# One load per tensor for each chunk of 1024 tokens, with a new written order of work

## The chip, the cores and the metric

The kernel runs on one core of a Trainium2 chip. A core has five engines that run side by side, each with its own list of instructions: PE (matrix products; its weight loads are shown apart, as PEld), DVE (vector), ACT (functions of one element), POOL (a second vector engine) and SP, which here only issues transfers. 16 DMA engines move data between device memory (HBM) and the core's memory (SBUF). PE writes its results to PSUM, a small memory of 8 banks of 2 KB for each of the 128 partitions. An engine takes its instructions strictly in order; an instruction whose input isn't there holds up all behind it on that engine. The metric is the time of one execution on the device in microseconds (us), as the median of several runs. One profiled execution shows where the time goes.

## The reference

The input is `x` with two gates, `r_gate` and `i_gate`, each of 4 sequences x 6336 tokens x 256 channels in float32, so 25,344 tokens in all. Two layers follow each other.

```python
sig_r, sig_i = sigmoid(r_gate), sigmoid(i_gate)
a_t  = exp(8 * sig_r * log(sigmoid(a_param)))          # one decay per token and channel
gx   = sqrt(max(1 - a_t * a_t, 1e-6)) * sig_i * x
for t in range(S):                                     # along each sequence
    h = a_t[:, t] * h + gx[:, t];  y[:, t] = h
gate = sigmoid(causal depthwise convolution of y with conv_w, 5 taps)
out  = (gate * (y @ w_val)) @ w_out                    # w_val, w_out: 256 x 256
```

## The kernel before

**Units.** Tokens are cut into 51 *tiles* (`wins`: 512 tokens, a few of 256) and the tiles are joined into 28 *chunks* (`CHUNKS`): the first three and the last two are single tiles, the 23 between are pairs, 1024 tokens. Channels are two halves of 128 (`h`). Pairs of chunks may form a *group* (`GROUPS`) for the transposes and Exp of the decay, and up to three chunks a *batch* (`BATCHES`) for the square roots.

**Layouts.** Loads put tokens on partitions: a tile of 512 tokens lies as 128 partitions x 4 tokens x 256 channels, four successive tokens in one partition, so one piece of a transfer is 4 x 256 x 4 bytes = 4 KB. The scan along the tokens needs channels on partitions, so PE transposes in between. Pairs of bf16 values travel as one float32 through such transposes.

**The steps.** Each has a two-letter name in the order; the line is that of the profile before.

- `lr`, `li`, `lx`: loads of the gates and of x, one tile and tensor each (512 KB), by SP (L274). Gates go to `riring` with places for 4 tiles (`NRI`), x to `xring` with 4 (`NX`).
- `th`: ACT takes Tanh of both gates of a tile at once into `tring` (bf16, L289). `tring` has 3 places (`NTRI`) of three parts: the i-gate always lies in the middle part and the r-gate alternates between the outer two (`swapped`), so that an r-part is overwritten only by the tile six later, an i-part by the tile three later.
- `tr`, `ex`: PE transposes the r-gate's Tanh (L334), ACT makes the decay from it by Exp into `aring` (L350).
- `sq` (or `sa` on ACT), `rt`: POOL squares the decay into `ering` (L358), ACT takes the square root of 1 - a^2 of a whole batch at once (L377). The square root needs another function table on ACT, so a batch costs two table loads (L509).
- `nt`, `xg`: PE transposes the root back to token layout (L392); DVE multiplies it into `uring` (L399).
- `pp` and `up` on POOL (L297, L309), or `xp` on PE with `uv` on DVE (L314, L323): the product of the i-gate and x, into `uring`.
- `xt`, `sc`: PE transposes the gated input to channel layout in PSUM (L408); DVE runs the scan into `yring` (L430).
- `cv`, `tg`: the convolution as 20 small products on PE (L442) and its Tanh on ACT (L449); `vl`, `gv`: the value product on PE (L457) and the gating on DVE (L462).
- `ou`, `cd` or `ca`, `st`: the output product on PE (L472), its copy to `oring` on DVE (L480) or ACT (L482), and the store by SP (L493).

In `nt`, the transposes of one tile pick every second float of `ering`, since a partition of token layout holds four successive tokens as two pairs; `xt` writes with the same step into PSUM:

```python
in_=ering[:, e + q:e + wins[w] // 2:nq]        # nt, nq = 2 for 512 tokens
out=bank[:, o + q:o + wins[w] // 2:nq]         # xt
```

**The order.** Nothing is scheduled by a compiler. The string `ORDER` lists every step (`th.7` is Tanh of tile 7; `tr.3.1@0,1` names PSUM banks), and the loop at L504 emits them one after the other, each to its engine. So each engine's list is the order of its own steps in the string; the place of a step relative to those of other engines has no effect beyond which data it must wait for. All loads and stores share SP's list: a store that waits for its copy holds up the loads behind it.

Of the kernel before, what the change touches and what calls it, by code (L numbers as in the profile page):

```python
# [26 lines left out]
NTRI = 3  # L27
# [6 lines left out]
s_ident s_small s_kt s_diag li.2 lr.2 th.2 lr.3 lr.0 li.0 th.0 pp.0 tr.2.0@0 li.1 lr.1 tr.0.0@1 ex.2.0 th.1 lx.0 lx.2  # L34
li.3 up.0 tr.2.1@2 ex.2.1 tr.0.1@0 ex.0.0 tr.1.1@3 ex.1.1 tr.1.0@4 sq.1.1 ex.0.1 sq.0.1 lx.3 xp.3@0,1 lx.1 lr.6 th.3
sq.0.0 rt.0 lr.5 sq.2.0 pp.2 up.2 nt.0@5 xg.0 xt.0@2,3 li.5 th.5 sq.2.1 li.6 lr.4 uv.3 th.6 pp.6 pp.5 xp.1@5 sc.0.0
sc.0.1 cv.0@2,3 uv.1 li.4 th.4 tg.0 s_wl.1 ex.1.0 lx.4 li.7 tr.3.1@0,1 s_wl.0 lr.7 ex.3.1 lx.5 tr.3.0@2,3 ex.3.0
s_wl.3 lx.6 lx.7 pp.4 up.4 th.7 lr.9 rt.2 xp.7@2,3 li.8 uv.7 sa.4.0 sq.4.1 sq.3.1 sq.1.0 rt.1 nt.2@0 xg.2 nt.1@1 xg.1
s_wl.2 lr.8 li.10 lx.8 xt.2@2,3 xt.1@0,1 sc.1.1 li.9 lr.10 sq.3.0 rt.3 li.11 up.6 sc.1.0 lx.10 lr.11 sc.2.1 sc.2.0
up.5 th.8 lx.11 s_wcast th.10 lx.9 pp.10 up.10 lr.14 th.9 li.13 li.14 lr.13 xp.8@4,5 li.12 lr.12 uv.8 th.11 li.15  # L40
nt.3@0,1 xg.3 nt.4@6,7 pp.11 up.11 cv.1@2,3 tg.1 xg.4 xt.3@0,1 sc.3.1 vl.1@4,5 tr.5.0@6,7 ex.5.0 sq.5.0 tr.5.1@2,3
gv.1 ou.1.0@1 cd.1.0 st.1 lx.12 lr.15 ex.5.1 vl.0@4,5 xp.9@6,7 th.14 sq.5.1 cv.2@2,3 sc.3.0 th.13 uv.9 lx.13 xt.4@1,0
gv.0 ou.0.0@4 cd.0.0 st.0 sc.4.1 lx.15 cv.3@6,7 th.12 li.16 li.18 tr.7.1@4,5 tg.2 vl.2@2,3 gv.2 tg.3 ex.7.1 sq.6.1
sq.6.0 lx.14 pp.14 pp.12 up.12 tr.7.0@6,7 ex.7.0 sq.7.0 lx.16 cv.4@2,3 tg.4 th.15 ou.2.0@4,5 cd.2.0 sc.4.0 st.2 lr.18
lr.16 vl.3@6,7 xp.13@2,3 vl.4@4,5 gv.4 sq.7.1 rt.4 uv.13 th.16 sq.8.1 sq.8.0 pp.15 up.15 li.17 lr.17 up.14 ou.4.0@4,5
li.19 cv.5@0,1 lr.19 gv.3 cd.4.0 lx.17 tg.5 ou.3.0@6,7 lx.18 st.4 cd.3.0 st.3 nt.5@4,5 li.20 xg.5 pp.16 up.16 th.17
pp.17 lr.20 nt.7@6,7 xg.7 lx.19 li.21 nt.6@2,3 xg.6 th.18 pp.18 lr.21 xt.5@4,5 sc.5.1 up.17 vl.5@6,7 cv.6@0,1 tg.6
th.19 tr.9.1@2,3 ex.9.1 li.22 lr.22 up.18 sq.9.1 pp.19 gv.5 sc.5.0 tr.9.0@6,7 ex.9.0 lx.20 ou.5.0@0,1 cd.5.0 sq.10.1
xt.6@5,4 up.19 sc.6.1 cv.7@0,1 tg.7 cv.8@2,3 th.20 lr.24 tg.8 sc.6.0 vl.6@6,7 gv.6 xt.7@0,1 cv.9@4,5 ou.6.0@6,7 sc.7.0
th.21 tg.9 cd.6.0 vl.7@2,3 gv.7 vl.9@6,7 th.22 tr.11.0@0 sc.7.1 ou.7.0@2,3 vl.8@4,5 sq.9.0 tr.12.0@1 gv.9 ou.9.0@6,7  # L50
gv.8 ou.8.0@4,5 sq.10.0 st.5 cd.7.0 cd.9.0 lx.22 st.6 rt.5 lx.21 nt.8@6,7 lr.23 li.23 cd.8.0 nt.9@4,5 pp.22 pp.21
up.22 pp.20 up.20 up.21 xg.8 ex.12.0 xg.9 ex.11.0 li.24 st.7 st.9 li.25 lr.25 lx.23 lx.24 li.26 lr.26 th.23 xt.8@6,7
sc.8.0 sq.11.0 pp.23 sq.12.0 lr.27 li.27 cv.11@2,3 tg.11 cv.10@4,5 sc.8.1 cv.12@0,1 st.8 th.24 pp.24 tg.10 tg.12
vl.11@2,3 tr.11.1@6 ex.11.1 gv.11 vl.10@4,5 gv.10 th.25 xt.9@0,1 sc.9.0 tr.12.1@2 ex.12.1 ou.11.0@6,7 cd.11.0
# [45 lines left out]
def kernel(  # L100
# [46 lines left out]

    segs, y_at, y_wrap = [], [], []
    at = 4
# [33 lines left out]
    with tc.manual_schedule():  # L183
# [79 lines left out]
        def swapped(w):  # L263

            return (w // NTRI) % 2

# [274 lines left out]
```

## Time and profile before

| | |
|---|---|
| median of 3 runs | 301.58 us (300.14 to 303.82) |
| profiled execution | 300.32 us, of which 298.5 us from the first to the last instruction (the span) |
| busy: ACT, DVE, PE, POOL | 278.8, 247.6, 246.4, 232.8 us |
| moved by DMA | 104.75 MB, 351 GB/s over the span |
| PE's granted clock | 0.977 of full speed |
| landing of a 512 KB load | 8.0 to 8.3 us after its issue (median) |

In the profile's groups, a line names the source line, engine and operation, the written and the read buffers, then busy time and mean duration, then the idle time of the engine just before these instructions with what ended most of it. Times in the slices are tenths of each fortieth of the span. The *chain that ended last* follows the work back from the last instruction: at each step to what released it. Its shares say where a delay would have moved the end.

### The profile page before, as it was taken

To read this page: it belongs to the slowest core of one execution; us is meant where nothing else is said; L and a number is where in the kernel's file an instruction comes from. 1 tells how busy PE (TensorE), PEld (TensorE's weight loads), DVE (VectorE), ACT (ScalarE), POOL (GpSimd) and SP (SyncE) were. 2 spreads that over 40 slices of the span, in tenths; PEclk is the share of its full clock that TensorE was granted. 3 is DMA by queue.
4 is the path that set the end of the run, shared out by engine and by line. 5 is a ranking of instruction groups with operands and counts; after the bars stand their busy time and mean duration, and the time that the engine had idled before them with its cause. 6 is when DMAs were issued, how large, how long until landed. Compare 5 with 4: busy or idle time off the path is not lost.

```text
span 298.5 us, 6286 instructions
## 1 busy us (share of the span) xinstructions
PE 246.4 (83%) x2509; PEld 167.8 (56%) x2509; DVE 247.6 (83%) x206; ACT 278.8 (93%) x197; POOL 232.8 (78%) x155
## 2 busy tenths in 40 slices
PE   0374577897888598989898899998979999899993
PEld 0134255454556466757664758567647675666662
DVE  2030288849999889999999999999999899899993
ACT  6799999999999999999999999999999999969863
POOL 1478958989999899899999879998995996255300
PEclk9997599999999979999999999999999999999999
DMA  6999999999999999999999998999999977726046
GB/s 252 408 408 385 379 411 407 406 414 406 337 379 370 419 416 415 411 406 321 417 411 375 388 417 335 396 353 361 349 409 419 408 278 270 273 116 248 29 186 246
DMA packets 29995, 104.75 MB, mean 351 GB/s; under 512 B 3335, under 2 KB 3854, under 8 KB 29966
## 3 DMA queue, kind: packets, MB, share of 16 engines
q1 hardware_dynamic: 29952, 104.35, 90.5%
q8 instruction: 19, 0.31, 0.4%
q14 instruction: 10, 0.08, 0.1%
q10 hardware_dynamic: 14, 0.01, 0.0%
HBM read 78.39 MB, written 25.95 MB: 350 GB/s over the span
## 4 chain that ended last, share of the span: by engine, by line
ACT 31%; PE 23%; DVE 13%; issue 13%; DMA 12%; POOL 5%; SPq 1%; ACTq 0%; DVEq 0%; POOLq 0%
ACT tring L289 10%; ACT aring L350 8%; DMA riring<-in_r_gate_dram 7%; DVE yring L430 7%; PE banks L442 5%; ACT tgring L449 5%; PE banks L457 5%; ACT ering L377 4%; PE banks L472 4%; PE banks L392 3%; DMA riring<-in_i_gate_dram 3%; DVE tgring L462 3%; DVE oring L480 2%; DMA xring<-in_x_dram 2%; ACT L509 2%
## 5 line engine op out<-in xcount | busy, mean ns | idle before, releaser
L430 DVE TENSOR_TENSOR_SCAN yring<-aring,yring,banks 128x1024 bf16<-128x1024 f32 (+5 forms) x54 | 106.2, 1988 | 0.9 <-PE banks L408 0.6
L358 POOL TENSOR_TENSOR ering<-aring 128x1024 f32<-128x1024 f32 (+2 forms) x54 | 91.5, 1713 | 9.7 <-ACT aring L350 9.7
L309 POOL TENSOR_TENSOR uring<-tring,xring 128x1024 bf16<-128x1024 bf16 (+1 forms) x45 | 94.6, 2113 | 4.9 <-DMA xring<-in_x_dram 3.5
L289 ACT ACTIVATE tring<-riring 128x2048 bf16<-128x2048 f32 (+1 forms) x51 | 93.8, 1867 | 4.1 <-DMA riring<-in_i_gate_dram 1.9
L297 POOL TENSOR_SCALAR tring<-tring 128x1024 bf16<-128x1024 bf16 (+1 forms) x45 | 45.8, 1026 | 30.5 <-ACT tring L289 30.4
L442 PE MATMUL banks<-yring,diag 64*64 64x512 bf16 (+7 forms) x1080 | 61.9, 361 | 4.6 <-ACT aring L350 1.6
L462 DVE SCALAR_TENSOR_TENSOR tgring<-tgring,banks 128x1024 bf16<-128x1024 bf16 (+1 forms) x51 | 58.9, 1178 | 5.5 <-PE banks L457 4.4
L472 PE MATMUL banks<-wo,tgring 128*128 128x256 bf16 x396 | 51.4, 274 | 4.7 <-DVE tgring L462 3.5
L350 ACT ACTIVATE aring<-banks,khf 128x2048 f32<-128x2048 bf16 (+3 forms) x38 | 54.1, 1474 | 0.5 <-PE banks L334 0.4
L449 ACT ACTIVATE tgring<-banks 128x1024 bf16<-128x1024 f32 (+1 forms) x51 | 50.4, 1009 | 3.4 <-PE banks L442 3.3
L457 PE MATMUL banks<-yring,wv 128*128 128x512 bf16 (+4 forms) x216 | 49.4, 361 | 5.0 <-DVE oring L480 2.2
L472 PEld LDWEIGHTS <-tgring 128*128 128x128 bf16 x396 | 41.0, 114 | 15.7 <-DVE tgring L462 9.6
L442 PEld LDWEIGHTS <-diag 64*64 64x64 bf16 x1080 | 30.3, 106 | 28.8 <-issue 13.6
L377 ACT ACTIVATE ering<-ering 128x4096 bf16<-128x4096 f32 (+5 forms) x15 | 44.9, 3019 | 0.1
L399 DVE TENSOR_TENSOR uring<-banks,uring 128x2048 bf16<-128x2048 bf16 (+2 forms) x28 | 29.8, 1095 | 18.2 <-PE banks L392 17.9
L480 DVE COPY oring<-banks 128x1024 f32<-128x1024 f32 (+1 forms) x35 | 40.6, 1181 | 4.8 <-ACT aring L350 2.4
L334 PE MATMUL banks<-ident_b,tring 128*128 128x128 bf16 x396 | 29.0, 227 | 12.2 <-ACT tring L289 10.4
L334 PEld LDWEIGHTS <-tring 128*128 128x128 bf16 x396 | 25.1, 101 | 17.7 <-ACT tring L289 11.7
L457 PEld LDWEIGHTS <-wv 128*128 128x128 bf16 x216 | 19.7, 97 | 26.3 <-issue 12.4
L392 PE MATMUL banks<-ident,ering 128*128 128x128 f32 x198 | 28.8, 296 | 6.8 <-DVE oring L480 2.6
L392 PEld LDWEIGHTS banks<-ident,ering 128*128 128x128 f32 x198 | 25.9, 208 | 13.5 <-ACT ering L377 7.7
L408 PE MATMUL banks<-ident,uring 128*128 128x128 f32 x198 | 27.5, 282 | 2.6 <-DVE uring L399 2.5
(36 smaller groups left out, 113.1 us busy)
## 6 DMA issues: line engine op xcount, KB each, us to landing
riring<-in_i_gate_dram SPq DMA_DIRECT2D x48, 512.0 KB, 8.2
riring<-in_r_gate_dram SPq DMA_DIRECT2D x48, 512.0 KB, 8.3
xring<-in_x_dram SPq DMA_DIRECT2D x48, 512.0 KB, 8.0
out_dram<-oring SPq DMA_DIRECT2D x48, 512.0 KB, 5.7
riring<-in_r_gate_dram SPq DMA_DIRECT2D x3, 256.0 KB, 6.3
riring<-in_i_gate_dram SPq DMA_DIRECT2D x3, 256.0 KB, 6.5
xring<-in_x_dram SPq DMA_DIRECT2D x3, 256.0 KB, 5.3
out_dram<-oring SPq DMA_DIRECT2D x3, 256.0 KB, 7.3
```

Of the source, the lines that this page charges most:

```text
L289: nc.scalar.activation(out=tring[:, w % NTRI, a:a + 2, 0:J, :], in_=riring[:, w % NRI, :, 0:J, :], func=ACT.Tanh, scale=0.5)
L309: nc.gpsimd.tensor_tensor(out=u, in0=t1, in1=xt, op=ALU.mult)
L350: nc.scalar.activation(out=dst, in_=src, func=ACT.Exp, scale=khf[:, h:h + 1], bias=khf[:, h:h + 1])
L358: nc.gpsimd.tensor_tensor(out=e, in0=a, in1=a, op=ALU.mult)
L377: nc.scalar.activation(out=ering[:].bitcast(BF16)[:, 4 * o:4 * o + 2 * n], in_=ering[:, 2 * o:2 * o + 2 * n], func=ACT.Sqrt, scale=-0.25, ...
L392: nc.tensor.transpose(out=bank[:, k:k + P], in_=ering[:, e + q:e + wins[w] // 2:nq], identity=ident[:])
L430: nc.vector.tensor_tensor_scan(out=yring[:, h, col:col + o1 - o0], data0=aring[:, h, a_at[c] + o0:a_at[c] + o1], data1=xT[:, o0:o1], initi ...
L442: nc.tensor.matmul(out=gp[oh * 64:oh * 64 + 64, h, a:b], lhsT=diag[half * 64:half * 64 + 64, h, k, :], rhs=yring[half * 64:half * 64 + 64, ...
L449: nc.scalar.activation(out=tgring[:, w % NTG, :, 0:wins[w]], in_=live.pop(("gp", w))[:, :, 0:wins[w]], func=ACT.Tanh, scale=0.5)
L457: nc.tensor.matmul(out=val[:, m, a:b], lhsT=wv[:, hk, m * P:(m + 1) * P], rhs=yring[:, hk, col:col + b - a], start=(hk == 0), stop=(hk == ...
L462: nc.vector.scalar_tensor_tensor(out=tgring[:, w % NTG, :, 0:wins[w]], in0=tgring[:, w % NTG, :, 0:wins[w]], scalar=1.0, in1=live.pop(("va ...
L472: nc.tensor.matmul(out=ops[:, j * D:(j + 1) * D], lhsT=gv[:, hk, j:wins[w]:J], rhs=wo[:, hk, :], start=(hk == 0), stop=(hk == H - 1))
```

## The change

Chunks, batches, groups and the arithmetic stay. Three things change.

1. A chunk of 1024 tokens is loaded whole: one transfer of 1 MB for each of r, i and x, eight successive tokens in one partition, so in pieces of 8 KB. The rings keep their size but are cut in two slots of a chunk each (two single tiles can share a slot). `th`, `up`, `uv` and `xp` still work by tile, on 4 of the 8 tokens of a partition. Inside a chunk the token order of `tr`/`ex`, `nt` and `xt` follows: the step in `nt`'s reads and `xt`'s writes becomes 4 floats.
2. `tring` has 5 places of two parts (r, i) instead of 3 of three; `swapped` goes.
3. `ORDER` is new throughout. By kinds: 84 loads of the three tensors instead of 153, four tiles instead of six go through `xp`/`uv` (the others through `pp`/`up`), 18 copies on ACT instead of 16 (33 instead of 35 on DVE), and the two `sa` are of 256 tokens each instead of one of 1024 and one of 256. All other counts are equal, among them 20 changes of the table.

```diff
-NTRI = 3
+NTRI = 5
 ORDER = """
-s_ident s_small s_kt s_diag li.2 lr.2 th.2 lr.3 lr.0 li.0 th.0 pp.0 tr.2.0@0 li.1 lr.1 tr.0.0@1 ex.2.0 th.1 lx.0 lx.2
...
+s_ident s_small s_kt s_diag li.0 lr.0 lr.1 th.0 li.1 th.1 tr.0.0@0 pp.0 tr.1.1@1 tr.1.0@2 lx.0 lx.1 lr.2 up.0 pp.1
...
+    ri_at = places(NRI, [len(z) for z in CHUNKS])
+    x_at = places(NX, [len(z) for z in CHUNKS])
...
-        riring = rings.tile([P, NRI, 2, 4, D], FP32, name="riring")
-        xring = rings.tile([P, NX, 4, D], FP32, name="xring")
-        tring = rings.tile([P, NTRI, 3, 4, D], BF16, name="tring")
+        riring = rings.tile([P, NRI // 2, 16, D], FP32, name="riring")
+        xring = rings.tile([P, NX // 2, 8, D], FP32, name="xring")
+        tring = rings.tile([P, NTRI, 2, 4, D], BF16, name="tring")
...
+        def gates_in(c):
+            at = ri_at[c]
+            slot = riring[:, at // 2]
+            if len(cwins[c]) == 1:
+                slot = slot[:, at % 2 * 8:at % 2 * 8 + 8]
+            return slot.rearrange("p (k j) d -> p k j d", k=2)
+
+        def x_in(c):
+            return xring[:, x_at[c] // 2, x_at[c] % 2 * 4:]
 
         def load(w, which):
-            n = wins[w]
-            J = n // P
+            c = chunk_of[w]
+            J = clen[c] // P
             if which == "x":
-                dst = xring[:, w % NX, 0:J, :]
+                dst = x_in(c)[:, 0:J, :]
             else:
-                dst = riring[:, w % NRI, "ri".index(which) ^ swapped(w), 0:J, :]
-            nc.sync.dma_start(dst, flat[which][wstart[w]:wstart[w] + n, :].rearrange("(p j) d -> p j d", p=P))
+                dst = gates_in(c)[:, "ri".index(which), 0:J, :]
+            nc.sync.dma_start(dst, flat[which][wstart[w]:wstart[w] + clen[c], :].rearrange("(p j) d -> p j d", p=P))
...
         def op_th(w):
             J = wins[w] // P
-            a = swapped(w)
-            nc.scalar.activation(out=tring[:, w % NTRI, a:a + 2, 0:J, :], in_=riring[:, w % NRI, :, 0:J, :],
+            j = (w - cwins[chunk_of[w]][0]) * J
+            nc.scalar.activation(out=tring[:, w % NTRI, :, 0:J, :], in_=gates_in(chunk_of[w])[:, :, j:j + J, :],
                                  func=ACT.Tanh, scale=0.5)
...
         def op_nt(c, *at):
             bank = banks[:, at[0]:at[-1] + 1].rearrange("p b n -> p (b n)")
-            k = 0
-            for w in cwins[c]:
-                nq = wins[w] // (2 * P)
-                o = live["n", c] + (wstart[w] - cstart[c]) // 2
-                for q in range(nq):
-                    for h in range(H):
-                        e = o + h * clen[c] // 2
-                        nc.tensor.transpose(out=bank[:, k:k + P], in_=ering[:, e + q:e + wins[w] // 2:nq], identity=ident[:])
-                        k += P
+            k, o, half = 0, live["n", c], clen[c] // 2
+            for q in range(half // P):
+                for h in range(H):
+                    e = o + h * half
+                    nc.tensor.transpose(out=bank[:, k:k + P], in_=ering[:, e + q:e + half:half // P], identity=ident[:])
+                    k += P
             live["nT", c] = bank[:, 0:k]
...
         def op_xt(c, *at):
+            half = clen[c] // 2
             for h in range(H):
                 bank = banks[:, at[h]]
+                k = 0
                 for w in cwins[c]:
-                    nq = wins[w] // (2 * P)
-                    o = (wstart[w] - cstart[c]) // 2
-                    for q in range(nq):
+                    for q in range(wins[w] // (2 * P)):
                         nc.tensor.transpose(
-                            out=bank[:, o + q:o + wins[w] // 2:nq],
+                            out=bank[:, k:half:half // P],
                             in_=uring[:, (w + 1) % NU, q, h * P:(h + 1) * P, :].rearrange("p d two -> p (d two)")
                             .bitcast(FP32),
                             identity=ident[:])
+                        k += 1
                 live["xT", c, h] = bank
```

More of the change, by code (lines that the diff above doesn't have):

```diff
@@ L39 @@
[L39 to L53, printed above, removed]
@@ L326, in op_tr @@
         def op_tr(c, h, *at):
[L327 to L328 removed]
+            cs = sorted(group_of[c], key=lambda k: a_at[k])
             bank = banks[:, at[0]:at[-1] + 1].rearrange("c k n -> c (k n)").bitcast(BF16)
[L330 to L336 removed]
+            for g, k in enumerate(cs):
+                j = 0
+                for w in cwins[k]:
+                    for i in range(wins[w] // P):
+                        o = (j * len(cs) + g) * P
+                        nc.tensor.transpose(out=bank[:, o:o + P], in_=tring[:, w % NTRI, 0, i, h * P:(h + 1) * P],
+                                            identity=ident_b[:])
+                        j += 1
             live["rT", c, h] = bank
```

131 lines of the change are left out of this document (66 added, 65 removed).

## The prediction

> **What bounds the kernel now.** I read the busy rows and slices first, then a window over the steady stage, then the groups with their waits, then the chain that ended last, and at the end the matrix engine's transposes one line at a time.
>
> ```profile
> PE 246.4 (83%) x2509; PEld 167.8 (56%) x2509; DVE 247.6 (83%) x206; ACT 278.8 (93%) x197; POOL 232.8 (78%) x155
> ...
> PE   0374577897888598989898899998979999899993
> ...
> ACT  6799999999999999999999999999999999969863
> ...
> DMA  6999999999999999999999998999999977726046
> GB/s 252 408 408 385 379 411 407 406 414 406 337 379 370 419 416 415 411 406 321 417 411 375 388 417 335 396 353 361 349 409 419 408 278 270 273 116 248 29 186 246
> ```
>
> ACT is full from slice 3 to slice 35; PE is full only in the last fifth; the DMA engines look full until slice 31.
>
> ```profile
> 60.00:240.00 180.00, 160.01 (x1696) 111.91 (x1699) 170.40 (x132) 179.11 (x115) 167.33 (x101) 0.99 1.00 387
> 250.00:298.00 48.00, 42.72 (x443) 28.51 (x440) 41.63 (x35) 35.83 (x33) 14.03 (x11) 1.00 0.49 189
> ```
>
> Columns: window, its length, then busy time of PE, PEld, DVE, ACT, POOL, granted clock, DMA share, GB/s. From 60 to 240 us ACT works 179.1 of 180 us: it sets the pace. But DVE (170.4), POOL (167.3) and PE (160.0) have 5 to 11% of slack each, so little may be added to any of them. From 250 us on, PE and DVE set it.
>
> Do loads hold ACT up?
>
> ```profile
> L289 ACT ACTIVATE tring<-riring 128x2048 bf16<-128x2048 f32 (+1 forms) x51 | 93.8, 1867 | 4.1 <-DMA riring<-in_i_gate_dram 1.9
> ```
>
> The gates' Tanh, the only ACT work that waits for a load, lost 4.1 us in 51 instructions, and the list of its waits puts 3.3 us of that down to DMA, all but 0.6 before 25 us. So the 1.00 of DMA share is a queue kept full by early requests, not a limit.
>
> **The change, part by part.**
>
> *Loads.* 153 loads become 84. The trace's packet records have 84 ns in the median for a 2 KB piece and 159 for a 4 KB one: 75 ns per 2 KB and 9 fixed, so an 8 KB piece is estimated at 309 against twice 159. Of 18,432 pieces of 4 KB all but those of two 512-token chunks join in pairs, about 8,800 times 9 ns over 16 engines, 5 us of DMA time. Since ACT waits for loads only at the start, I count nothing; what hides it is the 179.1 us of ACT work. [...]
>
> *Start.* The first Tanh needs 0.5 MB instead of 1 MB. Before, it started at 5.58 us after a wait of 0.83; the setup on ACT ends at 4.74, so the 0.8 us goes. What is late next is the third Tanh: 2.6 MB stand ahead of it now, and with 2.1 MB landed at 9.22 us (where the second Tanh started before) and 408 GB/s it starts near 10.5, an ACT wait of 2.7 us; two 8 KB pairs later some 1.6 more. That is 4.3 us against 3.3 before. I count 0; between -3.3 (no wait left) and +1.5.
>
> *ACT's list.* In the order, ahead of the square root of batch 10 (`rt.10`, 249.51 us before, the last point where ACT sets the pace) stand one short Tanh (1.05 us) and two short Exp (0.56 each) more than before, and one 1024 Square (1.04) is replaced by two of 256 (0.42 each). With the 0.1 us by which neighbours overlap this is **+1.6 us**. The 10 table switches stay 10. The 2 copies that move from DVE to ACT come after it, where ACT works 35.8 of 48 us: 0. From the first transpose after that root the PE work is alike: 10 gate convolutions, 10 value products, 12 output products, 5 + 5 transposes in both. Ahead of it stand 6.4 us of PE work instead of 4.7 beside the root's own 5.33 us: **+0.5** (0 to +1.1).
>
> *Vector or POOL for u.* Two tiles go from DVE's `uv` to POOL's `pp` and `up`: POOL +6.4 us (2 x (1.05 + 2.16)), and +1.3 from the squares; DVE -2.9, PE -3.9 (6 of 22 instructions, 14.4 us, of L314). All in the first 75 us; in the first 60 POOL works 41.7 and PE 33.7: 0. Without that cover POOL's part would be 7.7.
>
> *Rings.* The gates' bf16 ring keeps an i-part for five tiles instead of three (ACT waited 0.5 us for it), an r-part for five instead of six. The new wait is Tanh on the transpose five tiles back; in the list that transpose always stands ahead; in six places one of the Exp that read it comes after the Tanh, so that there alone the wait is new. Behind a waiting Tanh the whole of ACT stands, so it would cost in full; I take 0, at most 1 us in each.
>
> *Transposes.* In a chunk of 1024 the token order inside a partition now runs over 8 tokens, not 4. `nt` reads `ering` with a step of 4 floats (16 bytes), before 2 (8 bytes); `xt` writes PSUM with 4, before 2. The trace has steps 1 and 2:
>
> ```profile
> L392 PEld LDWEIGHTS banks<-ident,ering x198: 142/209/232, 17.9 to 281.5; 128*128 128x128 f32 x198
> ...
> L408 PEld LDWEIGHTS banks<-ident,uring x198: 138/141/231, 19.9 to 288.3; 128*128 128x128 f32 x198
> ```
>
> ```profile
> 264.43 1.04 PE L408 MATMUL banks<-ident,uring 128*128 128x128 f32 x8
> 265.30 1.12 PE L392 MATMUL banks<-ident,ering 128*128 128x128 f32 x8
> ```
>
> (The second line's 138/141 is `xt`, which loads contiguous floats; min/median/max in ns.) The same load takes 141 ns contiguous and 209 with step 2. In rows of eight the matmuls follow each other every 109 and 120 ns; the records of the loads show a second load 58 ns behind a first with step 1, 97 with step 2. So step 2 costs 39 ns of reading, of which 11 reach the pace because the matmul itself takes 109. Step 4 isn't in the trace. Below: 0, nothing more. Above: the whole load's growth doubled, 2 x 67 = 134 ns. I take twice 39, **about 80 ns**, nearest to the reading rows: 97 + 78 = 175 no longer hides behind 109. It hits 23 chunks x 8 = 184 transposes, 14.7 us of PE (0 to 24.7). PE has 20 us idle between 60 and 240 us, so part is covered. How much is not, the chain tells:
>
> ```profile
> by line: issue 13.4%; ACT tring L289 10.1%; ACT aring L350 7.6%; DMA riring<-in_r_gate_dram 6.6%; DVE yring L430 6.6%; PE banks L442 5.4%; ACT tgring L449 5.4%; PE banks L457 5.2%; ACT ering L377 4.3%; PE banks L472 4.2%; PE banks L392 3.2%
> ```
>
> L392 holds 3.2% of the chain, 9.6 us, of about 24 us that its 198 transposes take at 120 ns: 40% lie on the path, between the square root that releases them and the DVE product that waits (17.9 us in its waits). 40% of 14.7 is **+5.9 us**. In the last stretch alone 24 of them stand in a full PE. For `xt`'s writes I count 0: rows with step 1 and with step 2 go at the same 109 ns; at worst as much again as the reads.
>
> [...]
>
> *Sum.* Profiled execution 300.32 us (span 298.5 and 1.8 around it): + 1.6 + 0.5 + 5.9 = 308.3. It stands 1.3 below the median of the three runs, 301.58, which scatter over 3.7; 2% is about what a measurement of this kernel can tell from no change. Forecast: **308 us**.
>
> **Rivals.**
>
> *The step of 16 bytes costs nothing* (not slower): the load stays behind the matmul or PE's 20 idle us take it. For it: step 2 lost only 11 of 67 ns. Against it: the load now exceeds what the matmul hides. Then 300.3 + 2.1 = 302.4; with the median's offset 303.7. It decides below about 30 ns.
>
> *Loads do set the pace* (faster), so that the 5 us of DMA time and the 3.3 us of waits at the start go: 300.3 - 8.3 + 2.1 = 294. For it: DMA share 1.00 from 60 to 240 us. Against it: 3.3 us of waits in all, and the dips to 321 GB/s in the slices, which leave room. [...]
>
> *Coarse slots starve ACT* (slower): a gate slot is now 1024 tokens, and both loads of chunk c+2 wait for the second Tanh of chunk c. ACT's listed work between that Tanh and the first of c+2 is 8.5 us in the tightest place (tiles 28 to 31) and 10.4 to 11.4 in four more. The 2 MB take 5.1 us at 408 GB/s and 2.2 until landing (the first 1 MB before: issued at 0.72, used at 5.5, 2.6 of that moving). With 1 MB of x and a store queued ahead, 3.9, that is 11.2: short by 2.7 + 0.8 + 0.6 + 0.6, about 5 us; SP's stores ahead, which wait for copies, can add as much again. For it: the median landing of 8.2 us for 512 KB. Against it: tiles had as little as 8.1 us before without a wait. It adds to the forecast: 313, up to 318.
>
> **How the numbers follow.** Forecast 0.45; coarse slots 0.2; no cost of the step 0.25; loads 0.1. The low end 298 lies between the faster rival and the free step; the high end 318 takes in the full 134 ns at 40% (+9.9 instead of 5.9) with starved slots. Faster by over 2% (under 295.5) is the loads' rival, 0.1. Slower (over 307.6): 0.65 of the forecast's share, 0.29, all of the starved slots, 0.2, and a small share of the free step, 0.03: 0.52. Within: 0.38.
>
> **What would show it.** The weight loads of `nt` (L395 then) near 290 ns and over, against 209, with rows of eight at about 200 ns; `xt` still at 109; PE busy some 11 us up; DVE's product waiting more than 17.9 us for `nt`. ACT's last batch roots later than 249.5 by 1.6 plus what is lost in the middle. If `nt` stays at 120 ns the forecast is wrong by its main term; if Tanh waits over 5 us for DMA after 60 us, the slots are the cause.

## The result, and the profile after

| | kernel before | changed kernel |
|---|---|---|
| median time | 301.28 us (300.14 to 303.82, 4 runs) | 310.41 us (309.73 to 310.72, 4 runs) |
| profiled execution | 300.32 us | 309.73 us |
| its span | 298.5 us | 307.8 us |
| ACT busy | 278.8 us | 280.2 us |
| ACT idle in the span | 19.7 us | 27.6 us |

The changed kernel is slower: ratio 1.0288, 95% interval 1.022 to 1.0356. The forecast was 308 us, within 298 to 318. The number is close by luck: the term that made up most of it, 5.9 us, turns out to be worth nothing, and a rival that had 0.2 put a loss of nearly that size in its place. A kernel's time is the median of its runs; two runs of e1b, one of the experiments below, lay over 1.5% above its fastest and are left out.

The busy rows and the slices of the changed kernel, to be read against those of before:

```profile
PE 247.7 (80%) x2480; PEld 168.3 (55%) x2503; DVE 244.6 (79%) x201; ACT 280.2 (91%) x199; POOL 238.6 (78%) x159
...
PE   1214969688878898978995888998899999899993
...
ACT  6579999999999999999979999999899989879753
...
DMA  7999999999999999999999999989899946743344
GB/s 249 367 421 418 421 371 423 399 378 412 405 390 381 386 399 309 412 389 345 401 384 406 350 383 379 402 291 416 360 352 359 380 163 211 275 171 138 139 200 175
```

PE busy rose by 1.3 us, not by the 11 that the forecast asked for. ACT did 1.4 us more work and stood 7.9 us longer. The steady stage and the last stretch, 48 us from behind the root of batch 10 (window, length, busy time of PE, PEld, DVE, ACT, POOL, granted clock, DMA share, GB/s):

```profile
60.00:240.00 180.00, 156.47 (x1630) 109.31 (x1644) 167.43 (x127) 175.56 (x112) 160.43 (x96) 0.99 0.98 377
259.00:307.00 48.00, 42.22 (x423) 27.84 (x426) 38.53 (x32) 35.19 (x31) 20.12 (x16) 1.00 0.46 177
```

From 60 to 240 us *every* engine did less than before: ACT 175.56 instead of 179.11 us, PE 156.5 instead of 160.0, DVE 167.4 instead of 170.4, POOL 160.4 instead of 167.3. When all of them lose, none has become the bound; they wait for something outside. The groups that wait for loads say what (idle time before the group is the last part):

```profile
L318 POOL TENSOR_TENSOR uring<-tring,xring 128x1024 bf16<-128x1024 bf16 (+1 forms) x47 | 98.0, 2093 | 21.6 <-DMA xring<-in_x_dram 18.0
...
L293 ACT ACTIVATE tring<-riring 128x2048 bf16<-128x2048 f32 (+1 forms) x51 | 93.4, 1860 | 9.9 <-DMA riring<-in_i_gate_dram 4.4
```

POOL's product of i-gate and x (`up`) waited 18.0 us for x, Tanh 9.9 us in all (before 4.1). The product's line before had 3.5:

```profile
L309 POOL TENSOR_TENSOR uring<-tring,xring 128x1024 bf16<-128x1024 bf16 (+1 forms) x45 | 94.6, 2113 | 4.9 <-DMA xring<-in_x_dram 3.5
```

And the chain that ended last, which in the kernel before held no x load among its first eleven lines, now has one at 5.2%, with the POOL product that it releases at 4.6%:

```profile
by line: issue 10.0%; ACT tring L293 7.7%; DVE yring L434 7.2%; DMA riring<-in_r_gate_dram 7.1%; PE banks L446 6.1%; ACT ering L383 5.9%; DMA riring<-in_i_gate_dram 5.5%; DMA xring<-in_x_dram 5.2%; PE banks L476 5.0%; POOL uring L318 4.6%; 
```

Why the loads are late is seen on the queue of SP, which issues them. Its waits before (total us, times, longest; L274 are loads, L493 stores):

```profile
SPq L493 <- DVE oring L480: 64.1, 22, 8.3
SPq L493 <- ACT oring L482: 46.1, 15, 8.0
SPq L274 <- ACT tring L289: 20.1, 11, 4.8
SPq L274 <- POOL uring L309: 14.7, 6, 5.9
```

and after (L278 loads, L497 stores):

```profile
SPq L497 <- DVE oring L484: 94.9, 25, 10.6
SPq L278 <- ACT tring L293: 53.1, 14, 7.3
SPq L497 <- ACT oring L486: 47.4, 15, 7.0
SPq L278 <- POOL uring L318: 23.8, 8, 7.4
```

Loads now wait 76.9 us for the readers of their slots (Tanh and `up`) instead of 34.8, and stores 142 us for the copies of their output instead of 110. What is listed behind such a wait on SP goes out only after it, as the load of x at 233.56 us below does behind two stores.

One place shows how a late load reaches ACT. These are the issues of SP (start, duration) in the changed kernel:

```profile
224.28 0.42 SPq L278 DMA_DIRECT2D riring<-in_r_gate_dram  x1
224.76 0.47 SPq L278 DMA_DIRECT2D riring<-in_i_gate_dram  x1
232.64 0.82 SPq L497 DMA_DIRECT2D out_dram<-oring  x2
233.56 0.67 SPq L278 DMA_DIRECT2D xring<-in_x_dram  x1
```

and this is what POOL did next (start, duration, at the end the idle time before):

```profile
243.14 2.15 POOL L318 TENSOR_TENSOR uring<-tring,xring 128x1024 bf16<-128x1024 bf16 x1 [8.26 <-DMA xring<-in_x_dram]
245.25 3.74 POOL L364 TENSOR_TENSOR ering<-aring 128x1024 f32<-128x1024 f32 x2
248.96 2.16 POOL L318 TENSOR_TENSOR uring<-tring,xring 128x1024 bf16<-128x1024 bf16 x1
```

The x of tiles 43 and 44 goes to a slot whose last reader, `up.40`, started at 217.61 us and was done at 219.8. The load (`lx.43`) was issued at 233.56, because two stores ahead of it on SP waited for their copies until 232.62: the slot had long been free here, and the stores held the load. It is 1 MB, and its product started 9.6 us after the issue. POOL stood 8.26 us; behind `up.43` in its list are the squares of the last chunks of batch 10 (L364), which the root of that batch needs. The root started at 258.56 us, before at 249.51.

This place is not the whole loss. ACT itself stood only 1.3 us for it, the last two lines below; two waits of Tanh for a gate, the first two lines, cost it 2.7 us (tiles 34 and 44):

```profile
158.08 1.91 ACT L293 ACTIVATE tring<-riring 128x2048 bf16<-128x2048 f32 x1 [1.55 <-DMA riring<-in_i_gate_dram]
...
216.86 3.71 ACT L293 ACTIVATE tring<-riring 128x2048 bf16<-128x2048 f32 x2 [1.19 <-DMA riring<-in_r_gate_dram]
...
251.15 1.06 ACT L293 ACTIVATE tring<-riring 128x1024 bf16<-128x1024 f32 x1 [0.99 <-POOL uring L318]
...
258.56 5.33 ACT L383 ACTIVATE ering<-ering 128x6144 bf16<-128x6144 f32 x1 [0.30 <-POOL ering L364]
```

The third line is Tanh of tile 50, whose place in `tring` POOL's product of tile 45 had read until then; the fourth is the root.

### The profile page after: what moved, and what is told of

It is laid out like the page before. It is cut to its first block, busy times and chain, and to the rows that moved or that the text cites. A ratio compares the mean times of both kernels' runs of the same rounds, so it can differ in the third digit from the quotient of the medians.

```text
span 307.8 us, 6136 instructions
## 1 busy us (share of the span) xinstructions
PE 247.7 (80%) x2480; PEld 168.3 (55%) x2503; DVE 244.6 (79%) x201; ACT 280.2 (91%) x199; POOL 238.6 (78%) x159
## 3 DMA queue, kind: packets, MB, share of 16 engines
q1 hardware_dynamic: 20016, 104.34, 87.7%
## 4 chain that ended last, share of the span: by engine, by line
ACT 24%; PE 22%; DMA 18%; DVE 14%; issue 10%; POOL 9%; SPq 1%; ACTq 0%; DVEq 0%; POOLq 0%
ACT tring L293 8%; DVE yring L434 7%; DMA riring<-in_r_gate_dram 7%; PE banks L446 6%; ACT ering L383 6%; DMA riring<-in_i_gate_dram 6%; DMA xring<-in_x_dram 5%; PE banks L476 5%; POOL uring L318 5%; PE banks L461 5%; ACT aring L356 4%; DVE tgring L466 3%; DVE oring L484 3%; ACT tgring L453 3%; POOL tring L301 2%
## 5 line engine op out<-in xcount | busy, mean ns | idle before, releaser
L318 POOL TENSOR_TENSOR uring<-tring,xring 128x1024 bf16<-128x1024 bf16 (+1 forms) x47 | 98.0, 2093 | 21.6 <-DMA xring<-in_x_dram 18.0
L364 POOL TENSOR_TENSOR ering<-aring 128x1024 f32<-128x1024 f32 (+2 forms) x54 | 92.9, 1738 | 8.1 <-ACT aring L356 8.0
L446 PE MATMUL banks<-yring,diag 64*64 64x512 bf16 (+7 forms) x1080 | 64.8, 365 | 6.5 <-DVE uring L332 1.8
L301 POOL TENSOR_SCALAR tring<-tring 128x1024 bf16<-128x1024 bf16 (+1 forms) x47 | 47.6, 1021 | 16.2 <-ACT tring L293 16.1
L461 PE MATMUL banks<-yring,wv 128*128 128x512 bf16 (+4 forms) x193 | 48.2, 359 | 5.1 <-ACT tgring L453 3.0
L343 PE MATMUL banks<-ident_b,tring 128*128 128x128 bf16 x396 | 31.1, 234 | 23.3 <-ACT tring L293 17.0
L446 PEld LDWEIGHTS <-diag 64*64 64x64 bf16 x1080 | 29.2, 107 | 32.6 <-issue 17.8
L343 PEld LDWEIGHTS <-tring 128*128 128x128 bf16 x396 | 26.8, 105 | 30.8 <-ACT tring L293 20.0
L484 DVE COPY oring<-banks 128x1024 f32<-128x1024 f32 (+1 forms) x33 | 38.3, 1182 | 2.6 <-PE banks L476 2.1
L395 PE MATMUL banks<-ident,ering 128*128 128x128 f32 x198 | 31.1, 306 | 9.1 <-ACT ering L383 6.5
L395 PEld LDWEIGHTS banks<-ident,ering 128*128 128x128 f32 x198 | 27.4, 210 | 14.0 <-ACT ering L383 9.2
L461 PEld LDWEIGHTS <-wv 128*128 128x128 bf16 x216 | 19.6, 97 | 23.5 <-issue 9.8
```

Source lines behind the costliest of these rows:

```text
L318: nc.gpsimd.tensor_tensor(out=u, in0=t1, in1=xt, op=ALU.mult)
L364: nc.gpsimd.tensor_tensor(out=e, in0=a, in1=a, op=ALU.mult)
L395: nc.tensor.transpose(out=bank[:, k:k + P], in_=ering[:, e + q:e + half:half // P], identity=ident[:])
L446: nc.tensor.matmul(out=gp[oh * 64:oh * 64 + 64, h, a:b], lhsT=diag[half * 64:half * 64 + 64, h, k, :], rhs=yring[half * 64:half * 64 + 64, ...
L461: nc.tensor.matmul(out=val[:, m, a:b], lhsT=wv[:, hk, m * P:(m + 1) * P], rhs=yring[:, hk, col:col + b - a], start=(hk == 0), stop=(hk == ...
```

## The experiments

The kernel before took 300.8 to 301.7 us in the five series, so each time is given with its difference to the kernel before on the same chip in the same series. For the changed kernel that difference is +9.1 us.

| kernel | time, us | against before, us | ratio (95%) |
|---|---|---|---|
| changed kernel | 310.41 | +9.1 | 1.0288 (1.022 to 1.0356) |
| e3_steps_of_one | 310.02 | +8.3 | 1.0282 (1.025 to 1.0314) |
| e2_old_order_whole | 339.82 | +38.1 | 1.1245 (1.1165 to 1.1325) |
| e1_tile_loads | 305.79 | +4.1 | 1.0143 (1.0105 to 1.0181) |
| e10_tiles_whole_release | 309.34 | +8.5 | 1.029 (1.0229 to 1.035) |
| e11_x_by_tile | 307.15 | +6.2 | 1.022 (1.0142 to 1.0297) |
| e12_gates_by_tile | 309.81 | +8.8 | 1.0292 (1.0227 to 1.0358) |
| e5_stores_unheld | 305.44 | +3.7 | 1.0123 (1.0078 to 1.0168) |
| e6_tiles_and_unheld | 300.94 | -0.8 | 0.9976 (0.9946 to 1.0006) |
| e7_before_unheld | 298.50 | -3.2 | 0.9892 (0.9851 to 0.9934) |
| e4_half_stores | 306.17 | +5.3 | 1.0158 (1.0111 to 1.0205) |
| e8_whole_loads_hoisted | 328.32 | +26.6 | 1.0867 (1.0798 to 1.0936) |
| e1b_tile_loads_hoisted | 321.8 | +20.1 | 1.0664 (1.0563 to 1.0764) |

The theory after the result was that the whole chunk's slot delays the loads; the rivals were the step of 16 bytes (the forecast's own main term), the new order's content, and full DMA engines.

A second table says where the time goes. The forecast took the root of batch 10 for the last point where ACT sets the pace, and the traces bear it out: from its start to the end of the kernel nearly the same 49 us pass before and after the change. So a kernel's time is settled by ACT's work ahead of that root and by ACT's idle time there, which the table splits at the root of batch 4 (at 68.82 us before, 72.38 after). All are us, from one profiled execution of each kernel (the three far slower ones are left out):

| kernel | ACT's work ahead of the root of batch 10 | idle before the root of batch 4 | idle between the two roots | from the root of batch 10 to the end |
|---|---|---|---|---|
| before | 242.5 | 6.1 | 0.9 | 49.0 |
| changed | 244.6 | 8.2 | 5.7 | 49.3 |
| e3, steps of one | 244.1 | 8.4 | 6.5 | 48.9 |
| e1, all by tile | 244.6 | 8.8 | 1.7 | 49.1 |
| e10, release of the whole slot | 244.8 | 8.6 | 4.7 | 52.1 |
| e11, x by tile | 244.0 | 9.1 | 2.4 | 49.3 |
| e12, gates by tile | 244.4 | 9.6 | 3.8 | 49.3 |
| e5, stores unheld | 244.3 | 8.2 | 3.4 | 46.2 |
| e6, tiles and unheld | 244.2 | 9.1 | 0.9 | 46.2 |
| e7, before unheld | 242.5 | 5.8 | 1.6 | 46.9 |
| e4, half stores | 244.4 | 9.1 | 3.7 | 48.3 |

The span grew by 9.3 us with the change: 2.1 are work, 2.1 idle time up to the root of batch 4, 4.8 idle time between the roots, and 0.2 lie behind.

### Does the step of 16 bytes cost anything? (e3)

```diff
-nc.tensor.transpose(out=bank[:, k:k + P], in_=ering[:, e + q:e + half:half // P], identity=ident[:])
+nc.tensor.transpose(out=bank[:, k:k + P], in_=ering[:, e + q * P:e + q * P + P], identity=ident[:])
...
-    out=bank[:, k:half:half // P],
+    out=bank[:, k * P:k * P + P],
```

> The changed kernel, with the transposes of the root reading contiguous floats and the transposes of the gated input writing contiguous floats; the tokens of a chunk are thereby multiplied in a wrong order, everything else is equal. By the prediction's main term (80 ns on each of 184 transposes, 40% on the path): 6 us come back, 304.5. If the step costs nothing, as the changed kernel's trace shows (212 against 209 ns): 310 +- 1; the weight loads of the root's transposes fall to 141 ns all the same, since even the old step of 8 bytes had 209.

The weight loads of `nt` (min/median/max ns) in the changed kernel, beside those of `xt`, and two rows of eight matmuls:

```profile
L395 PEld LDWEIGHTS banks<-ident,ering x198: 138/212/231, 28.1 to 293.2; 128*128 128x128 f32 x198
...
L411 PEld LDWEIGHTS banks<-ident,uring x198: 138/140/224, 32.0 to 296.9; 128*128 128x128 f32 x198
```

```profile
266.56 1.09 PE L411 MATMUL banks<-ident,uring 128*128 128x128 f32 x8 [0.18 <-DVE uring L402]
271.41 1.12 PE L395 MATMUL banks<-ident,ering 128*128 128x128 f32 x8
```

The median load went from 209 ns with a step of 8 bytes to 212 with 16. A row of eight still takes 1.12 us, as before. Contiguous reads in e3 bring the load to 141 ns, yet the median moves by less than a microsecond, within the runs' scatter:

```profile
L395 PEld LDWEIGHTS banks<-ident,ering x198: 137/141/231, 28.9 to 293.3; 128*128 128x128 f32 x198
```

So nearly all of the load lies behind the matmul at either step: the transposes of `nt` follow each other every 120 ns before, 121 after and 109 in e3. The term of 5.9 us falls. `xt`'s writes to PSUM with a step of 4 floats cost nothing that shows: its transposes follow each other every 109 ns (median) at steps 1, 2 and 4 alike.

### Slots without the order, order without the slots (e2, e1)

e2 keeps the order of before and takes the new layout with one load per chunk and tensor; each load stands at the earlier of its two tiles' places, or directly behind the reading of its slot. The r-parts and i-parts of `tring` keep the depth of before (six and three). Only the x of one pair (tiles 3 and 4) stays loaded by the tile.

```diff
-x_at = places(NX, [len(z) for z in CHUNKS])
+x_at = [0, 1, 2, None] + [2 if c % 2 == 0 else 0 for c in range(4, len(CHUNKS))]
```

> The other half: the order of before, with the changed kernel's loads (1 MB per chunk and tensor at the place of the earlier of the two tile loads, or as soon after it as the slot is free), token layout and steps; the r-parts of the bf16 ring keep their depth of six and the i-parts three. Chunk 3 alone loads x by tile, since the old list uses its first tile very early. If the coarse slots cost the time: 305 to 308 us. If the new list costs it: 301 +- 1.5. If the 16-byte step costs it: 306 or more, with transposes of the root at about 200 ns.

It took 339.82 us, 38 more than before and far above the 305 to 308 expected of coarse slots. Its window and its Tanh:

```profile
60.00:240.00 180.00, 146.24 (x1435) 102.30 (x1451) 147.41 (x114) 157.53 (x99) 146.54 (x88) 0.92 0.87 338
```

```profile
L298 ACT ACTIVATE tring<-riring 128x2048 bf16<-128x2048 f32 (+1 forms) x51 | 93.4, 1857 | 39.3 <-DMA riring<-in_i_gate_dram 19.9
```

ACT works 157.5 of 180 us, and Tanh waits 31.5 us for the two gates (19.9 and 11.6). So the coarse slots starve ACT in this list far more than in the new one. How much of the 38 us is the slots' own is open: where each load stands in the list was my choice here, and part of the loss may be that choice.

e1 is the opposite: the changed kernel, its order and its layout, but with two transfers of 512 KB for each tensor of a chunk, the tile that is used first ahead.

```diff
-li.43 ... lr.43 ... lx.43
+li.44 ... lr.44 li.43 lr.43 ... lx.43 lx.44
...
-nc.sync.dma_start(dst, flat[which][wstart[w]:wstart[w] + clen[c], :].rearrange("(p j) d -> p j d", p=P))
+w0, J = cwins[c][0], wins[w] // P
+j = (w - w0) * J
...
+src = flat[which][wstart[w0]:wstart[w0] + clen[c], :].rearrange("(p j) d -> p j d", p=P)
+nc.sync.dma_start(dst[:, j:j + J, :], src[:, j:j + J, :])
```

> The changed kernel with its own order, rings and token layout, but each chunk of 1024 tokens loaded by two transfers per tensor (one tile of 512 tokens each, 512 KB in 4 KB pieces, the tile that is used first ahead), each waiting for the release of its own half of the slot. If the coarse slots cost the time (one landing and one release for two tiles), 4 to 6 us of the 9 come back: 304 to 306 us, and the waits for x before the product on POOL (18.0 us) and for the gates before Tanh (8.3 us) fall by half. If the new list itself costs it, whatever the size of a load, it stays at 310 +- 1.5. If the read with a step of 16 bytes costs it (the main term of the prediction), 310 as well.

305.79 us: of the 9.1 us 5.0 come back (4.4 by the ratios), 4.1 stay. The idle time between the two roots falls from 5.7 to 1.7 us; ACT's work and the idle time at the start don't fall. In its steady stage ACT is nearly as full as before the change, 178.34 against 179.11 us:

```profile
60.00:240.00 180.00, 159.15 (x1660) 110.97 (x1676) 170.86 (x132) 178.34 (x114) 161.17 (x97) 0.99 1.01 385
```

The waits did not fall by half, as expected: Tanh's for the gates went from 8.3 to 7.1 us, and the *sum* of POOL's waits for x did not fall at all (19.6 us). What fell is the wait at the place shown above, where `up.43` now starts at 239.39 us instead of 243.14: the two loads went out at 231.53, 2.0 us sooner than the whole one, and the product started 7.9 us after that instead of 9.6. A sum of waits on an engine that isn't the bound is a poor measure; their place decides.

### Landing or release? (e10)

In these kernels a 1 MB transfer differs from two of 512 KB in two ways: its first tile is used only when all of it has landed (`up.43` starts 9.6 us after the issue in the changed kernel, 7.9 in e1), and it is issued only when the whole slot has been read (in the changed kernel 2.7 to 3.6 us after the last reader's end, in the mean). e10 separates them. It loads by the tile like e1 (the edit is shown beside e1's), but the halves of a slot take turns, so that a chunk's first tile goes where the chunk before was read last; Tanh and the products read from the same turned place.

```diff
+G_TURN = "0000010110001010011011011100"
+X_TURN = "0000010101010000100001001000"
+def turned(w, turn):
+    c = chunk_of[w]
+    return (w - cwins[c][0] + int(turn[c])) % len(cwins[c]) * (wins[w] // P)
-nc.sync.dma_start(dst[:, j:j + J, :], src[:, j:j + J, :])
+at = turned(w, X_TURN if which == "x" else G_TURN)
+nc.sync.dma_start(dst[:, at:at + J, :], src[:, j:j + J, :])
```

> The changed kernel with tile transfers of 512 KB as in e1_tile_loads (305.79), but the halves of a slot are taken in turn, so that a chunk's first tile goes into the place that the chunk before read last: no load of a slot can start before all of the slot is read, as with the 1 MB transfers (310.41), and only the landing is by the tile. Everything is computed. If the loss of whole-chunk loads is the landing of 1 MB (a first tile waits for the second's bytes): the time stays with the tile transfers, 305 to 306.5. If it is the release (nothing starts until the second tile is read): 309 to 310.5. Between the two, each has its share: 4.6 us over the shares.

309.34 us, +8.5: all but half a microsecond of e1's gain is gone, and ACT's window is close to that of the changed kernel:

```profile
60.00:240.00 180.00, 155.61 (x1625) 109.08 (x1639) 167.74 (x127) 175.26 (x112) 160.31 (x96) 0.99 1.00 378
```

It is the release of the slot, not the landing. (e10's profiled execution was 2.9 us above its median; the second table shows them behind the root of batch 10, 52.1 us instead of 49. Ahead of it the idle time between the roots is 4.7 us again.) Worked out from the traces, as the time from the end of a slot's last reader to the issue of its load: before, a load's place stood free for 6.0 (r), 6.2 (i) and 7.7 us (x) in the mean until SP came to it; in the changed kernel 2.7, 3.0 and 3.6 us. So the places of before were free further ahead of their loads, a reserve against delays on SP's queue. But this mean alone doesn't tell a good kernel from a bad one: in e10 it is 5.4, 5.7 and 7.2 us, since the second tile's place is free early, and 3.4, 4.1 and 5.3 for the first tile's load alone.

### Which slot? (e11, e12)

e11 loads x by the tile; e12, with `whole = which == "x"`, the gates.

```diff
-J = clen[c] // P
+whole = which != "x"
+J = (clen[c] if whole else wins[w]) // P
```

> The changed kernel with x alone loaded by the tile (two transfers of 512 KB a chunk); both gates stay whole, 1 MB. Everything is computed. With all three tensors by tile it was 305.8, with none 310.4. If the whole x slot, whose release waits for POOL's second gating product, is what costs: most of the 4.6 us comes back, 306 to 307.5, and the gating products wait less for x than 18.0 us. If the gates' slots cost, as the prediction's rival had it (Tanh waits, ACT stands): 309 to 310.5.

> The counterpart: both gates loaded by the tile, x whole, 1 MB. Everything is computed. If the gates' slots cost: 306 to 307.5, and Tanh's waits for DMA after 60 us (2.7 us) go. If the x slot costs: 309 to 310.5, the gating products' waits for x stay near 18 us. If it is neither alone but the queue that they share, both kernels give back about half, 307.5 to 309.

x by the tile gives 3.0 us back, the gates by the tile 0.3; their intervals overlap, so the ranking is likely rather than proved. Tanh's waits for gates after 60 us went from 2.7 to 0.5 us in e12 and to 1.9 in e11. In the second table x by the tile takes 3.3 of the 4.8 us between the roots, the gates 1.9; e12 has 1.4 us more idle time than the changed kernel before the root of batch 4, which hides most of its gain (one profiled execution of each). The traces agree on x: the product `up.43` of e11 and that of e12,

```profile
240.11 2.16 POOL L320 TENSOR_TENSOR uring<-tring,xring 128x1024 bf16<-128x1024 bf16 x1 [6.62 <-DMA xring<-in_x_dram]
```

```profile
242.49 2.15 POOL L321 TENSOR_TENSOR uring<-tring,xring 128x1024 bf16<-128x1024 bf16 x1 [5.57 <-DMA xring<-in_x_dram]
```

and the root of batch 10, which needs the squares behind it, line up over these kernels:

| kernel | `up.43` starts, us | root of batch 10, us | apart |
|---|---|---|---|
| changed | 243.14 | 258.6 | 15.4 |
| e12, gates by tile | 242.49 | 257.9 | 15.4 |
| e11, x by tile | 240.11 | 255.5 | 15.4 |
| e1, all by tile | 239.39 | 255.0 | 15.6 |

In e10 they don't (241.40 and 258.2): its root came with ACT's own list, not with the squares.

Both kernels had the steady stage nearly restored (ACT 177.8 us in e11, 178.4 in e12): up to the root of batch 9 both had gained the same, at 225.6 and 225.8 us against 227.3. That freeing either tensor relieves SP's queue for the other would explain it, but is not shown. e12 loses its gain again at 242 us, where x is late: its root of batch 10 comes 2.4 us after that of e11.

### What stores do on the same queue (e5, e6, e7)

In e5 stores read a constant tile of zeros, so they wait for no copy; the traffic stays, the output is left out (`oring` gives up one of its four places for the tile).

```diff
-oring[:, w % NOSB, 0:J, :])
+still[:, 0:J, :])
```

> The changed kernel, with every store reading a constant tile instead of the output ring (so the output is not the product; the copies still run, into three places instead of four): same bytes and same list on SP, but no store waits for its copy, and no copy for a store. If the loads come late because stores that wait for copies stand ahead of them in SP's list (142 us of such waits in the changed kernel): 304 to 307 us. If they come late because a slot is free only after both of its tiles: 309 to 310.5.

e6 is this edit on e1, e7 the same edit on the kernel before.

> The changed kernel with both edits that gave time back: each chunk's tensors loaded by two transfers of 512 KB, one a tile (305.79 alone), and stores that read a constant tile, so that they hold nothing on SP's queue (305.44 alone); the output is left out by that, zeros are stored. If the whole-chunk transfers and the held stores are two separate losses: 310.4 - 4.6 - 5.0 = 300.8, and Tanh's and the gating products' waits for loads (7.1 and 19.6 us with tile loads, 8.6 and 16.3 with free stores) fall to the level of the kernel before (4.1 and 3.5). If both edits cure the same late landings: 304 to 305.5. If the rest of the loss is the new order's own work ahead of the Sqrt batches, the waits for loads fall away and it still stays above 304.

> The kernel before with the edit of e5_stores_unheld alone (stores read a constant tile, zeros are stored, the output is left out). If the 5 us that free stores gave the changed kernel belong to the change (loads that need a whole chunk's place come late behind stores), the kernel before gains only what lies behind its last gate: under 2 us, 299.5 to 301.5. If they are what any order of this kernel gains without the wait and the last store's landing, it gains the same: 296 to 297.

e5 gives 5.4 us back, e6 9.9. 5.0 from the tile loads and 5.4 from free stores would add up to 10.4, as if they were two separate losses. But part of what free stores give is a trait of the edit: the control e7 is 3.2 us faster than the kernel before too, more than the first reading of it allowed and less than the second, and its roots start no earlier (the last at 279.0 us, in the kernel before at 278.6). What its profiled execution gained lies behind the last root (17.8 us from there to the end instead of 19.9), where no store waits for the last copies; that is no cost of the change. In e5 and e6 the stretch behind the root of batch 10 is shorter by 3.1 us likewise (46.2 against 49.3).

What is left is the added idle time between the roots, 4.8 us. Free stores alone take 2.4 of it, tile loads alone 4.1, both together all of it. So the two overlap: most of what stores ahead of loads cost is gone once loads go by the tile. (e5's share may be smaller: its profiled execution was 1.6 us under its median.) In e5 the last root came earlier too, 279.3 against 282.0 us, and a free slot waited 1.6 to 1.8 us for its load, in the changed kernel 2.7 to 3.6.

With both edits the changed kernel still stands 2.4 us above the kernel before with free stores (300.94 and 298.50; 3.6 between the profiled executions). By the table that is the new order's own content: 1.7 us more work on ACT and 3.3 more idle time before the root of batch 4, less 1.4 later on.

### Are the DMA engines full? (e4)

```diff
-... "(p j) d -> p j d", p=P), oring[:, w % NOSB, 0:J, :])
+... "(p j) d -> p j d", p=P)[:, 0:J // 2, :], oring[:, w % NOSB, 0:J // 2, :])
```

> The changed kernel, of each tile only half the tokens stored (the rest of the output is left out): 13 MB of the 104 MB less, 51 stores wait for the same copies at the same places. If the late landings come of DMA engines that are full (98% to 99% busy through 240 us, 1 MB landing after 9 to 10 us): the loads land sooner, Tanh's and the gating products' waits fall by a third or more, and the time by 4 us or more, to 306.5 or below. If they come of slots released late and of loads held behind stores on SP's queue: the waits stay near 9.9 and 18.0 us, and the time at 309 to 310.5.

The time lies 3.8 us below the changed kernel, beside the 4 or more that full engines were to bring; 0.9 us of that lies behind the root of batch 10 (48.3 against 49.3). The waits fell less than a third: Tanh's for the gates from 8.3 to 8.4 us (nothing), the products' for x from 18.0 to 14.6. The slots stood free for as long as in the changed kernel (2.7, 3.0 and 3.6 us), so SP's queue hadn't changed. The DMA share between 60 and 240 us was 0.89, so the engines did get room, and the last root moved from 282.0 to 280.6. This one is undecided: full engines may have some share. The idle time between the roots fell by 2.0 us, less than by the tile loads' 4.1.

### Loads moved ahead of stores (e8, e1b)

If stores hold loads up, the loads could stand ahead of them in SP's list: in e8, 54 of the 1 MB loads stand directly behind the last reader of their slot, in e1b each load of e1 behind the last reader of its tile's place.

```diff
-st.32 st.33 lx.43
+lx.43 ... st.32 st.33
```

> The changed kernel, its 1 MB loads moved up in SP's list: 54 of them stand directly behind the last instruction that reads their slot, which takes them past 67 places of a store (31 loads pass one to four stores each). Everything is computed. If stores that wait for copies ahead of loads are a cause: SP's loads issue as soon as the slot is free, the waits of Tanh and of the gating products fall by a third as with free stores, and the time by 2 to 4 us, 306.5 to 308.5. If only the release of a whole slot and the landing of 1 MB count, the loads can't start sooner: 309.5 to 310.5. If stores now stand behind loads that wait for slots and the copies wait for the stores' places: above 311.

> The changed kernel with tile transfers of 512 KB (305.79), moved up in SP's list to directly behind the last reader of their own tile's place, so that a first tile's place is filled while the slot's other tile is still in use. Everything is computed. If the half of the loss that tile transfers left is again late loads behind stores and behind the other tile: 301 to 303.5. If it is the order's own content: 305 to 306.5, with fewer waits for loads. If early loads get in the stores' way: above 307.

Both became far slower, 328.3 and 321.8 us. In e8 the loads do go out sooner (1.2 to 3.1 us after their slot is free), but the stores take longer to land:

```profile
out_dram<-oring SPq DMA_DIRECT2D x48, 512.0 KB, 7.8
```

(5.0 us to landing in the changed kernel, 5.7 before. They also go out 1.4 us after their copies, up from 0.3; but before the change that was 1.3, without harm.) DVE's copies to `oring` waited 7.0 us for stores, which don't appear among their waits in the changed kernel. Three pieces of its chain are stores for whose place in `oring` a copy waited:

```profile
131.83 14.30 DMA out_dram<-oring
...
176.26 13.87 DMA out_dram<-oring
...
240.12 11.55 DMA out_dram<-oring
```

`oring` has four places; in the 7.0 us of those waits DVE stood, and with it the scan and everything behind. So in the changed kernel's list it costs less that stores hold loads up (310.4 us) than the other way round (328.3).

## Why the prediction was right in its number and wrong in its reason

- **Transposes, +5.9 us: the step that failed.** It took the 39 ns that a step of 8 bytes adds between two loads, doubled them for 16, and set 97 + 78 = 175 ns against the matmul's 109. The load didn't grow: 212 ns against 209, rows at 1.12 us as before, and e3 puts the whole at less than 1 us by the medians. DVE's product waited 8.1 us for `nt`, not over 17.9. The two points of the trace (141 ns contiguous, 209 at step 2) were stretched to a line; the third point, 212 at step 4, shows a plateau. The first rival, "the step of 16 bytes costs nothing", was right on this.
- **Coarse slots starve ACT, about 5 us, given 0.2: this is what happened**, at 4.4 to 5.0 us by e1 and e10; the profiled executions have 4.8 us more idle time between the roots. Its price was right, its path only half of it. The rival followed the gates' slots to Tanh, and there ACT lost 2.7 us (tiles 34 and 44). It had no term for x, whose lateness reaches ACT through POOL: 1.9 us of waits for POOL between the roots, and x by the tile gives more back than the gates (e11 against e12). Its rider, that stores ahead on SP can add as much again, was right in kind, but the two don't add: free stores alone take 2.4 of the same 4.8 us.
- The sign given in advance, "if Tanh waits over 5 us for DMA after 60 us, the slots are the cause", would have acquitted them: it was 2.7 us. It watched one of two loads' users, and set the mark above what Tanh lost.
- **ACT's list +1.6 and PE's work +0.5:** ACT's work ahead of the root of batch 10 rose by 2.1 us (1.5 to 2.3 in the other kernels of the table with this order), and the stretch behind it by 0.2. Both terms held in size.
- **Start 0, up to +1.5: over its bound.** The third Tanh started at 10.45 us, as worked out (10.5), but a later one waited 2.7 for its r-gate where 1.6 was expected. Up to 60 us Tanh waited 5.5 us for gates instead of 3.3. The root of batch 4 came 3.6 us later, with 1.4 us more ACT work and 2.1 more idle time ahead of it. Neither tile loads nor free stores cure that (8.8 and 8.2 us idle in the table), so it goes with the new order; which part of that causes it, no run shows.
- **Loads 0:** 8 KB pieces take 309 ns in the median, as estimated, but the 5 us did not come. Slow pieces lift the mean to 337 ns, twice the 168 of a 4 KB piece, and the queue's time is what it was: 90.5% of 298.5 us before, 87.7% of 307.8 after, 270 us in both. Throughput in the steady stage fell from 387 to 377 GB/s. The rival that loads set the pace through their bytes fell. The two 512 KB transfers of e1 moved 385 GB/s in the same stretch, and the kernel was 5.0 us faster with them.
- **Rings, `xt`, POOL for u, at 0:** one wait of Tanh for the five-deep ring's i-part, 1.0 us (tile 50, behind the late x), and none over 0.6 us for its r-part; `xt` at 109 ns a transpose; no loss seen by POOL's extra products in the first 60 us.

In sum, of the 9.3 us by which the profiled span grew, 2.1 are work on ACT, 2.1 the start, 4.8 the coarse slots, in part together with stores held ahead of loads, and 0.2 lie behind the root of batch 10. The forecast had 1.6, 0, 0 and 0.5 for these and 5.9 for the transposes: it came near because 5.9 us that weren't there stood for the slots and the start. A version faster than the kernel before did not come out of these runs: the only ones below it store no result.

## What to carry to other kernels

Here a larger transfer was also a larger unit of release: with the same 512 KB transfers, a kernel that could start none before the whole slot was read took 309.3 us, one that could took 305.8. So before merging loads, work out for each slot when its last reader ends, what stands ahead of its load in the queue, and when the data is first used. Follow every user of a load to the engine list behind it, not only the bottleneck's own; here a second vector engine's wait of 8.26 us for x delayed the squares that the bottleneck needed. And in a queue that loads and stores share, moving one ahead of the other can cost more than it gains (328 and 322 us here), so look at what waits for the side that is moved back.

## What the hardware showed that was not expected

- A float32 weight load of 128 x 128 reads with a step of 8 or 16 bytes at the same 209 to 212 ns (141 contiguous), and a row of transposes goes at 120 or 121 ns each against 109.
- Two kernels whose PE worked less between 60 and 240 us were granted a lower clock there: 0.92 in e2 (146 us busy) and 0.94 in e8 (151 us), against 0.99 before and after (160 and 156 us). A part of their 38 and 27 us may be that; it wasn't separated.
